# Merging the values and scores of the paired attention phase into one interruption of the feed-forward stream

## The chip, the cores and the metric

One core of one Trainium2 chip runs the whole program. The metric is the device time of one execution in microseconds (us). The median of three runs of the kernel before is 897.06 us (896.87 to 897.44). In the profiled execution TensorE had its full clock (2.4 GHz, granted clock 0.999).

## The reference

Banded attention over 8 batches, 8 heads, 576 positions and a head size of 64, followed by a two-layer feed-forward block with a leaky ReLU:

```python
scores = (1 / sqrt(64)) * q @ k.T          # [8, 8, 576, 576]
mask = (0 <= i - j) & (i - j < 64)         # each query sees itself and 63 keys before it
attn = softmax(where(mask, scores, -1e9))  # the sum has 1e-9 added
x = (attn @ v).transpose(0, 2, 1, 3).reshape(4608, 512)
h = x @ w_in                               # [4608, 2048]
out = maximum(0.01 * h, h) @ w_out         # [4608, 512]
```

All inputs and the output are float32.

## The kernel before, in words

**Units and pairs.** The 8 batches times 9 blocks of 64 queries are 72 units. A unit holds all 8 heads; it needs the 64 keys of its own block and the 64 before them. Two neighbouring units make a pair, numbered m = 0 to 35. Four pairs make one chunk of 512 rows of x, so there are nine chunks c = 0 to 8.

**The feed-forward stream.** For each chunk c and each of 16 tiles f of the hidden dimension, `mm1` (L532) computes h in 12 matmuls of 128x128 by 128x512: x and w_in are each split into a high and a low fp32r part, and three products are summed over four blocks of 128. It hands back three steps. `leak` (ScalarE, L544) writes the leaky ReLU g, `high` (ScalarE, L550) writes its high part gh, and `low` (VectorE, L554) writes gl = g - gh. `mm2` (L570) then adds gh and gl times w_out into four accumulator banks, 12 matmuls in four triples (gh, gh, gl). In the stream `mm2` of one step stands behind `mm1` of the next, so the three steps have the length of one `mm1` to finish. After f = 15 the four accumulators are evicted (L592) and stored.

**The paired phase.** Chunks 0 to 2 need pairs 0 to 11, which are done in earlier phases. From chunk 2 on a loop runs over n = 0 to 111, one (c, f) each. Pairs 12 to 35 are computed inside it, two pairs (m, m+1) in each eight steps, which I call a turn. TensorE leaves the stream twice per turn; I call each such interruption a visit:

- At the second step of a turn (at == 1): `scores_3` (L465) of both pairs. They are fp32 matmuls on 64x64 tiles of the array, two banks for each pair. `shield_3` (L470, VectorE) scales and masks them into e, `most_3` (L482, GpSimd) takes column maxima with partition_all_reduce, `exps_3` (L489) subtracts them (VectorE) and takes the exponential (ScalarE). The maximum of (m, 1) and that of (m+1, 0) are written to the two halves of `late_n`, the other two to a spare tile.
- At the third and fifth steps: exps of m+1, the sums by partition_all_reduce (L495, GpSimd; they too go to `late_n` and the spare tile), and `fold_3` (L499, VectorE), which makes reciprocals in `late_n`.
- At the sixth step (at == 5): `values_3` (L505) of both pairs, fp32 matmuls in 128x64 column tiles, one bank each ("s" for the even pair, "t" for the odd). `product_3` (L518) multiplies the bank by the reciprocals into `late_n` (VectorE) and copies the high part to x (ScalarE). `low_3` (L523, VectorE) writes the low part of x.

**Banks.** PSUM has eight banks: four accumulators o0 to o3, the two that `mm1` takes in turn ("o" and "h"), and "s" and "t". Before the change the scores of an even pair go to "s" and "t", those of an odd pair to "o" and "h".

**Order.** At the end a loop ties each instruction to the one written before it on the same engine ("issue order"). So every engine runs its instructions in the order of the program text; a wait at the head of an engine's queue holds all behind it. Tiles free their buffers by dependencies that the framework derives: a matmul that writes a bank waits until the last reader of its old content is done.

What stands in the loop at the visits of the kernel before:

```python
        if at == 5:
            for x in (m, m + 1):
                values_3(x)
                load_v(x + 2)
            product_3(m)
            fold_3(m + 1)
            low_3(m)
...
        if at == 1:
            for x in (m, m + 1):
                scores_3(x)
                load_q(x + 2)
```

Of the kernel before, what the change touches and what calls it, by code (L numbers as in the profile page):

```python
# [28 lines left out]
NU = B * NQB  # L29
# [5 lines left out]
PAIRED = 12  # L35
# [48 lines left out]
def flat(t):  # L84
    return t.rearrange("p a b -> p (a b)") if len(t.shape) == 3 else t
# [3 lines left out]
def band_attention_ffn(ctx: ExitStack, tc: tile.TileContext, qT, kB, vW, vL, w_in, w_out, eye_mask, out):  # L89
# [9 lines left out]
    def bank(tag, name):  # L99
        return ps_e.tile([P, 512], F32, tag=tag, name=name)  # L100


    of_h, of_a = cycle("oh"), cycle("st")
# [23 lines left out]
    def k_of(m):  # L127
        if m >= PAIRED:
            return (ks[0], later.get("k"), ks[1])[(m - PAIRED) % 3]
        return more[:, m] if m in (2, 3) else ks[m % 2]  # L130

    def v_of(m):
        if m >= PAIRED:
            return (vs[0], later.get("v"))[m % 2][:, :, : H * D]
        return vs[m % 2 if m < TURNED // 2 else 0][:, :, : H * (D + 1)]
# [8 lines left out]
    def load_k(m):  # L144
        if m < NU // 2:
            nc.sync.dma_start(k_of(m), kB[m])

    def load_v(m):
        if m < NU // 2:
            nc.sync.dma_start(v_of(m), vL[m - PAIRED] if m >= PAIRED else vW[m])  # L150
# [94 lines left out]
    def mask_of(u):  # L245

        kinds = [v % NQB == 0 for v in (u, u + 1)]
        if any(kinds):
            return away[:, 1:] if kinds[0] else away[:, :2]
        return away[:, :1]  # L250
# [204 lines left out]
    def open_room():  # L455

        e, n, v = (wk.tile([P, 512, 2], U32, tag="raw", bufs=3, name=f"late_{x}") for x in "env")
        e, n, v = (flat(x).bitcast(F32).rearrange("p (a b) -> p a b", a=2) for x in (e, n, v))
        k = flat(wk.tile([P, NP, 2, D], F32, tag="y", bufs=1, name="late_k").rearrange("p a b c -> p a (b c)"))
        later.update(e=e, n=n, v=v, k=k.rearrange("p (a b c) -> p a b c", a=UNITS, b=NP))  # L460

    def e_of(m):
        return (probs_of, later["e"])[m % 2]

    def scores_3(m):  # L465
        ps = [bank(t, f"s{m}_{j}") for j, t in enumerate((next(of_h), next(of_h)) if m % 2 else "st")]
        quarter_scores(m, ps, False)
        probs[m] = ps

    def shield_3(m):  # L470
        ps = probs.pop(m)
        a = mask_of(UNITS * m).bitcast(F32)
        n = a.shape[1]
        a = flat(a)[:, None, :].broadcast_to([P, H // n, n * QB])
        for j in range(2):
            e, s = (x.rearrange("a (b c) -> a b c", c=n * QB) for x in (e_of(m)[:, j], ps[j]))
            nc.vector.scalar_tensor_tensor(e, s, SCALE, a, ALU.mult, ALU.add)  # L477

    def spare(name):
        return wk.tile([P, 512], F32, tag="pT", bufs=1, name=name)  # L480

    def most_3(m):  # L482
        for j in range(2):
            b = 2 * (m % 2) + j
            mx = later["n"][:, b - 1] if b in (1, 2) else spare(f"mx{m}_{j}")
            nc.gpsimd.partition_all_reduce(mx, e_of(m)[:, j], P, ReduceOp.max)  # L486
            probs[m, j] = mx

    def exps_3(m):  # L489
        for j in range(2):  # L490
            e = e_of(m)[:, j]
            nc.vector.tensor_tensor(e, e, probs.pop((m, j)), ALU.subtract)  # L492
            nc.scalar.activation(e, e, AF.Exp)  # L493
# [5 lines left out]
    def fold_3(m):  # L499
        r, t = later["n"][:, m % 2], probs.pop((m, "sum"))  # L500
        nc.vector.tensor_scalar_add(r[64:], t[64:], 1e-9)
        nc.vector.tensor_scalar_add(r[:64], r[:64], 1e-9)
        nc.vector.reciprocal(r, r)  # L503

    def values_3(m):  # L505
        ps = bank("st"[m % 2], f"o{m}")
        for w in range(UNITS):
            v = v_heads(m, w)
            for p in range(NP):
                for j in range(2):  # L510
                    c = (2 * p + w) * QB
                    nc.tensor.matmul(  # L512
                        ps[64 * j : 64 * j + 64, c : c + QB], v[:, 2 * p + j], e_of(m)[:, j, c : c + QB],
                        start=True, stop=True,
                    )
        probs[m] = ps

    def product_3(m):  # L518
        r = later["n"][:, m % 2]
        nc.vector.tensor_tensor(r, probs.pop(m), r, ALU.mult)  # L520
        nc.scalar.copy(x_of(UNITS * m)[0], r.rearrange("a (b c) -> a b c", b=NP))

    def low_3(m):  # L523
        hi, lo = x_of(UNITS * m)
        t = later["n"][:, m % 2].rearrange("a (b c) -> a b c", b=NP)
        nc.vector.tensor_tensor(lo, t, hi.bitcast(F32), ALU.subtract)
# [5 lines left out]
    def mm1(c, f, part):  # L532

        xh, xl = xs[c]
        ps = bank(next(of_h) if c or f >= half else "h", f"h{c}_{f}_{part.start}")[:, part]
        wh, wl = wi[f]
        terms = [(a, b, k) for k in range(KT) for a, b in ((wh, xh), (wh, xl), (wl, xh))]
        for n, (a, b, k) in enumerate(terms):
            nc.tensor.matmul(ps, a[:, k, :], b[:, k, part], start=n == 0, stop=n == len(terms) - 1)  # L539
        t = []  # L540

        def leak():
            t.append(wk.tile([P, CH], F32, tag="g", bufs=1, name=f"g{c}_{f}_{part.start}")[:, part])
            nc.scalar.activation(t[0], ps, AF.Prelu, alpha=0.01)  # L544

        def high():
            g[c, f, part.start] = [
                wk.tile([P, CH], F32R, tag=n, name=f"{n}{c}_{f}_{part.start}") for n in ("gh", "gl")
            ]
            nc.scalar.copy(g[c, f, part.start][0][:, part], t[0])  # L550

        def low():
            hi, lo = (x[:, part] for x in g[c, f, part.start])
            nc.vector.tensor_tensor(lo, t[0], hi.bitcast(F32), ALU.subtract)  # L554

        return leak, high, low

    acc, sums, due = {}, {}, []
# [11 lines left out]
    def mm2(c, f, part):  # L570


        gh, gl = g.pop((c, f, part.start))
        wh, wl = wo[f]
        for i in range(part.start // P, part.stop // P):
            split = c == 1 or c == 0 and i < 2
            begin = f == 0 or split and f == half
            end = f == FT - 1 or split and f == half - 1
            if begin:
                pool, tag = (ps_o, f"o{i}")  # L580
                if c == 1 and f == 0 and i > 1:
                    pool, tag = ps_e, "st"[i - 2]
                acc[c, i] = pool.tile([P, DM], F32, tag=tag, name=f"acc{c}_{i}_{f}")
            ts = slice(i * P, (i + 1) * P)
            for n, (a, b) in enumerate(((gh, wh), (gh, wl), (gl, wh))):
                nc.tensor.matmul(  # L586
                    acc[c, i], a[:, ts], b, start=begin and n == 0, stop=end and n == 2
                )
            if end:
                due.append(partial(evict, c, i, f, split))  # L590
# [24 lines left out]
    def flush():  # L615
        while due:
            due.pop(0)()

    whole, first, second = slice(0, CH), slice(0, CH // 2), slice(CH // 2, CH)
# [40 lines left out]
    prev = jobs[-1]  # L660
    jobs = [(c, half + k, whole) for c in range(2) for k in range(half)]
    first_late = len(jobs) - UPC - 3
    for n, job in enumerate(jobs):
# [25 lines left out]
        prev = job  # L689

    open_room()
    load_k(PAIRED + 1)
    load_v(PAIRED + 1)
    steps = [(c, f) for c in range(2, NCHUNK) for f in range(FT)]
    for n, (c, f) in enumerate(steps):
        m = PAIRED + n // 8 * 2
        at = n % 8 if m < NU // 2 else None
        for step in mm1(c, f, whole):  # L700
            step()
        if at == 2:
            exps_3(m + 1)

            nc.vector.memset(later["n"][:1, 0, :1], 0.0)
            sums_3(m, 0)
            sums_3(m, 1)
            sums_3(m + 1, 0)
        if at == 4:
            fold_3(m)  # L710
            sums_3(m + 1, 1)
        if at == 5:
            for x in (m, m + 1):
                values_3(x)
                load_v(x + 2)
            product_3(m)
            fold_3(m + 1)
            low_3(m)
        if at == 6:
            product_3(m + 1)  # L720
            low_3(m + 1)
        if prev:
            mm2(*prev)
            flush()
        prev = (c, f, whole)
        if at == 1:
            for x in (m, m + 1):
                scores_3(x)
                load_q(x + 2)
            load_k(m + 2)  # L730
            load_k(m + 3)
            shield_3(m)
            shield_3(m + 1)
            most_3(m)
            exps_3(m)
            most_3(m + 1)
            mm2(*prev)
            flush()
            prev = None
# [61 lines left out]
```

## Time and profile before

| what | value |
|---|---|
| median of 3 runs | 897.06 us |
| profiled execution, its own time | 898.25 us |
| its span, first to last instruction | 896.5 us |
| TensorE matmuls busy | 887.8 us, 99% |
| VectorE busy | 498.6 us, 56% |
| ScalarE busy | 304.2 us, 34% |
| GpSimd busy | 315.1 us, 35% |
| DMA | 68.48 MB, mean 76 GB/s |

A row of the timeline gives the start, the duration, the engine, the line of the kernel, the operation, what it writes and reads, and how many equal neighbours were merged into the row. Times are us from the span's start. Matmuls overlap in the array: the start of one follows the start of the last by less than its duration, so distances are to be read from start to start. A bracket at the end tells how long the engine had been idle and what ended that.

### The profile page before, as it was taken

What the parts mean: (1) busy time and instruction counts of PE and PEld (TensorE: products, weight loads), DVE (VectorE), ACT (ScalarE), POOL (GpSimd) and SP (SyncE); (2) the same over time, 40 slices, a digit from 0 to 9 for tenths busy, and PEclk for the clock granted to TensorE, in tenths of its full rate; (3) what the DMA queues carried; (4) which work ended last, traced back from release to release, by engine and by line L of the source; (5) the groups of instructions that cost most, each with busy time, mean ns of one, the idle gap of its engine ahead of it and who ended that gap; (6) DMA issues with size and microseconds to landing.
All of it is one profiled execution on the core that took longest, in us unless ns stands there. A gap on an engine that the chain in (4) does not pass through costs nothing.

```text
span 896.5 us, 16193 instructions
## 1 busy us (share of the span) xinstructions
PE 887.8 (99%) x7018; PEld 730.0 (81%) x7018; DVE 498.6 (56%) x650; ACT 304.2 (34%) x517; POOL 315.1 (35%) x132
## 2 busy tenths in 40 slices
PE   8999999999999999999999999999999999999998
PEld 5887888888888888888888888888888888888886
DVE  7999774587473636455464737373636455461111
ACT  4666554232232333223322232223323322323222
POOL 5332000674351708071625335351708071620000
PEclk9999999999999999999999999999999999999999
DMA  9764633233311111012211121112101211001001
GB/s 317 216 211 120 222 89 123 72 101 128 116 48 36 59 50 59 35 48 71 72 48 48 48 95 48 48 49 89 53 4 59 81 48 48 2 1 48 0 1 48
DMA packets 30359, 68.48 MB, mean 76 GB/s; under 512 B 3024, under 2 KB 3152, under 8 KB 30288
## 3 DMA queue, kind: packets, MB, share of 16 engines
q1 hardware_dynamic: 25824, 51.75, 16.9%
q10 hardware_dynamic: 4464, 15.70, 5.9%
q8 instruction: 55, 0.90, 0.4%
q14 instruction: 16, 0.13, 0.0%
HBM read 56.43 MB, written 11.01 MB: 75 GB/s over the span
## 4 chain that ended last, share of the span: by engine, by line
PE 98%; issue 0%; POOL 0%; DMA 0%; ACT 0%; DVE 0%; ACTq 0%; DVEq 0%
PE acc L586 45%; PE h L539 44%; PE s L239 4%; PE o L512 3%; PE o L328 1%; DMA k<-kB 0%; PE s L273 0%; PE t L354 0%; PE o L424 0%; PE s L307 0%; POOL mx L293 0%; POOL room L293 0%; DVE s L603 0%; DVE e L283 0%; ACT e L314 0%
## 5 line engine op out<-in xcount | busy, mean ns | idle before, releaser
L539 PE MATMUL h<-x,wi 128*128 128x512 f32 (+1 forms) x1440 | 337.1, 384 | 0.5 <-ACT g L544 0.5
L539 PEld LDWEIGHTS h<-x,wi 128*128 128x128 f32 x1440 | 265.5, 188 | 54.5 <-ACT g L544 0.7
L586 PE MATMUL acc<-wo,gh 128*128 128x512 f32 x936 | 292.7, 394 | 0.5 <-DVE s L603 0.5
L554 DVE TENSOR_TENSOR gl<-g,gh 128x512 fp32r<-128x512 f32 (+1 forms) x147 | 107.5, 731 | 330.6 <-ACT gh L550 330.2
L586 PEld LDWEIGHTS acc<-wo,gh 128*128 128x128 f32 x936 | 172.8, 188 | 37.1 <-DVE s L603 0.7
L544 ACT ACTIVATE g<-h 128x512 f32<-128x512 f32 (+1 forms) x147 | 86.3, 587 | 328.8 <-PE h L539 325.2
L586 PE MATMUL acc<-wo,gl 128*128 128x512 f32 x468 | 182.5, 390 | 0.0
L486 POOL PARTITION_ALL_REDUCE mx<-e x12 | 21.4, 1782 | 307.0 <-DVE e L477 307.0
L586 PEld LDWEIGHTS acc<-wo,gl 128*128 128x128 f32 x468 | 87.8, 188 | 18.6
L550 ACT CAST gh<-g 128x512 fp32r<-128x512 f32 (+1 forms) x147 | 90.0, 612 | 10.6 <-PE acc L586 6.3
L503 DVE RECIPROCAL late_n<-late_n 128x512 f32<-128x512 f32 x24 | 80.5, 3352 | 0.8
L539 PE MATMUL h<-x,w 128*128 128x512 f32 x324 | 77.8, 389 | 0.0
L539 PEld LDWEIGHTS h<-x,w 128*128 128x128 f32 x324 | 60.8, 188 | 12.6
L586 PE MATMUL acc<-w,gh 128*128 128x512 f32 x216 | 66.7, 390 | 0.0
L497 POOL PARTITION_ALL_REDUCE late_n<-e x12 | 38.8, 3233 | 25.6 <-ACT late_e L493 25.6
L493 ACT ACTIVATE e<-e 128x512 f32<-128x512 f32 x24 | 15.2, 633 | 95.4 <-DVE e L492 95.4
L393 POOL PARTITION_ALL_REDUCE mx<-e x8 | 15.2, 1899 | 91.5 <-DVE e L385 88.2
L586 PEld LDWEIGHTS acc<-w,gh 128*128 128x128 f32 x216 | 40.5, 188 | 8.4
L586 PE MATMUL acc<-w,gl 128*128 128x512 f32 x108 | 42.0, 389 | 0.0
L293 POOL PARTITION_ALL_REDUCE mx<-e x13 | 25.7, 1978 | 45.1 <-ACT e L285 28.1
L497 POOL PARTITION_ALL_REDUCE n<-late_e x12 | 41.5, 3460 | 0.0
L497 POOL PARTITION_ALL_REDUCE late_n<-late_e x12 | 40.9, 3408 | 0.0
(99 smaller groups left out, 825.8 us busy)
## 6 DMA issues: line engine op xcount, KB each, us to landing
q<-qT SPq DMA_DIRECT2D x34, 256.0 KB, 3.5
raw<-w_out ACTq DMA_DIRECT2D x15, 512.0 KB, 3.6
out<-o SPq DMA_DIRECT2D x30, 256.0 KB, 2.1
raw<-w_in ACTq DMA_DIRECT2D x14, 512.0 KB, 3.7
k<-kB SPq DMA_DIRECT2D x25, 256.0 KB, 3.7
v<-vL SPq DMA_DIRECT2D x12, 512.0 KB, 3.8
late_v<-vL SPq DMA_DIRECT2D x12, 512.0 KB, 4.2
v<-vW SPq DMA_DIRECT2D x8, 520.0 KB, 5.3
```

Of the source, the lines that this page charges most:

```text
L239: nc.tensor.matmul(ps[j][t, c : c + QB], k[i][s, p], q[s, w, p], start=not begun and (not more or (w, p) == (0, 0)), stop=not begun and no ...
L293: nc.gpsimd.partition_all_reduce(mx, probs[b], P, ReduceOp.max)
L393: nc.gpsimd.partition_all_reduce(mx, probs_of[:, j], P, ReduceOp.max)
L486: nc.gpsimd.partition_all_reduce(mx, e_of(m)[:, j], P, ReduceOp.max)
L497: nc.gpsimd.partition_all_reduce(t, e_of(m)[:, j], P, ReduceOp.add)
L503: nc.vector.reciprocal(r, r)
L512: nc.tensor.matmul(ps[64 * j : 64 * j + 64, c : c + QB], v[:, 2 * p + j], e_of(m)[:, j, c : c + QB], start=True, stop=True,)
L539: nc.tensor.matmul(ps, a[:, k, :], b[:, k, part], start=n == 0, stop=n == len(terms) - 1)
L544: nc.scalar.activation(t[0], ps, AF.Prelu, alpha=0.01)
L550: nc.scalar.copy(g[c, f, part.start][0][:, part], t[0])
L554: nc.vector.tensor_tensor(lo, t[0], hi.bitcast(F32), ALU.subtract)
L586: nc.tensor.matmul(acc[c, i], a[:, ts], b, start=begin and n == 0, stop=end and n == 2)
```

## The change

One visit takes the values of two pairs and then the scores of the next two. The turns are shifted so that the visit stands two steps ahead of a multiple of eight (n = 14, 22, ..., 86). The first turn keeps its two visits (scores at n = 1, values at n = 5), n = 6 has scores alone, n = 94 values alone. The banks of the scores are exchanged: an even pair now takes "o" and "h", an odd pair "s" and "t", which the values of the visit have just filled. At f == 0 the call of `mm2` for the step before and two of its four evictions are written after the matmuls of `mm1` and ahead of its `leak`, `high` and `low`.

```diff
     def scores_3(m):
-        ps = [bank(t, f"s{m}_{j}") for j, t in enumerate((next(of_h), next(of_h)) if m % 2 else "st")]
+        ps = [bank(t, f"s{m}_{j}") for j, t in enumerate("st" if m % 2 else (next(of_h), next(of_h)))]
...
     for n, (c, f) in enumerate(steps):
-        m = PAIRED + n // 8 * 2
-        at = n % 8 if m < NU // 2 else None
-        for step in mm1(c, f, whole):
+        turn_of = (n + 2) // 8 if n > 5 else 0
+        m = PAIRED + 2 * turn_of
+        at = n - (8 * turn_of - 2 if turn_of else 1)
+        two = (m, m + 1) if m < NU // 2 else ()
+        mine = mm1(c, f, whole)
+        if f == 0:
+            mm2(*prev)
+            prev = None
+            for _ in range(2):
+                due.pop(0)()
+        for step in mine:
             step()
-        if at == 2:
+        flush()
+        if at == 1 and two:
             exps_3(m + 1)
...
-        if at == 4:
+        if at == 3 and two:
             fold_3(m)
             sums_3(m + 1, 1)
-        if at == 5:
-            for x in (m, m + 1):
+        if n == 5:
+            for x in two:
                 values_3(x)
                 load_v(x + 2)
             product_3(m)
             fold_3(m + 1)
             low_3(m)
-        if at == 6:
-            product_3(m + 1)
-            low_3(m + 1)
+        elif at == 5 and two:
+            fold_3(m + 1)
+        if n == 6:
+            product_3(m - 1)
+            low_3(m - 1)
         if prev:
             mm2(*prev)
             flush()
         prev = (c, f, whole)
-        if at == 1:
-            for x in (m, m + 1):
+        if at == 0 and m <= NU // 2:
+            done = (m - 2, m - 1) if turn_of > 1 else ()
+            for x in done:
+                values_3(x)
+                load_v(x + 2)
+            for x in two:
                 scores_3(x)
                 load_q(x + 2)
-            load_k(m + 2)
-            load_k(m + 3)
-            shield_3(m)
-            shield_3(m + 1)
-            most_3(m)
-            exps_3(m)
-            most_3(m + 1)
+            for x in two:
+                load_k(x + 2)
+            for x in done:
+                product_3(x)
+            for x in two:
+                shield_3(x)
+            for x in done:
+                low_3(x)
+            if two:
+                most_3(m)
+                exps_3(m)
+                most_3(m + 1)
             mm2(*prev)
             flush()
             prev = None
```

## Rows read from the trace of the kernel before

**Rows 1.** The page's chain that ended last, by engine.
```profile
PE 98%; issue 0%; POOL 0%; DMA 0%; ACT 0%; DVE 0%; ACTq 0%; DVEq 0%
```

**Rows 2.** Timeline of TensorE around a scores visit: start us, us, engine, line, operation.
```profile
429.27 0.39 PE L586 MATMUL acc<-wo,gl 128*128 128x512 f32 x1
429.59 0.27 PE L239 MATMUL s<-q,late_k 64*64 64x64 f32 x2
...
431.62 0.73 PE L586 MATMUL acc<-wo,gh 128*128 128x512 f32 x2
...
434.47 5.60 PE L539 MATMUL h<-x,wi 128*128 128x512 f32 x24
...
477.60 0.27 PE L239 MATMUL s<-q,k 64*64 64x64 f32 x2
```

**Rows 3.** Timeline of TensorE around the values visit of the same turn.
```profile
448.07 2.88 PE L539 MATMUL h<-x,wi 128*128 128x512 f32 x12
450.88 1.15 PE L512 MATMUL o<-e,v 128*64 128x64 f32 x32
451.87 1.10 PE L512 MATMUL o<-late_e,late_v 128*64 128x64 f32 x32
452.90 0.73 PE L586 MATMUL acc<-wo,gh 128*128 128x512 f32 x2
```

**Rows 4.** Timeline of TensorE in an earlier phase: values, then scores, of one pair.
```profile
171.14 1.15 PE L424 MATMUL o<-e,v 128*64 128x64 f32 x32
172.22 1.16 PE L239 MATMUL s<-q,k 64*64 64x64 f32 x64
173.31 0.74 PE L586 MATMUL acc<-w,gh 128*128 128x512 f32 x2
```

**Rows 5.** Timeline of VectorE behind the scores visit of rows 2.
```profile
430.80 1.29 DVE L477 SCALAR_TENSOR_TENSOR e<-s,away 128x512 f32<-128x512 f32 x2 [1.85 <-PE s L239]
432.01 1.28 DVE L477 SCALAR_TENSOR_TENSOR late_e<-s,away 128x512 f32<-128x512 f32 x2
433.48 1.53 DVE L492 TENSOR_TENSOR e<-e,mx 128x512 f32<-128x512 f32 x1 [0.19 <-POOL mx L486]
435.24 1.53 DVE L492 TENSOR_TENSOR e<-e,late_n 128x512 f32<-128x512 f32 x1 [0.23 <-POOL late_n L486]
438.74 0.69 DVE L554 TENSOR_TENSOR gl<-g,gh 128x512 fp32r<-128x512 f32 x1 [1.96 <-ACT gh L550]
```

**Rows 6.** Timeline of ScalarE behind the scores visit of rows 2.
```profile
436.81 0.63 ACT L493 ACTIVATE e<-e 128x512 f32<-128x512 f32 x1 [1.13 <-DVE e L492]
437.45 0.60 ACT L544 ACTIVATE g<-h 128x512 f32<-128x512 f32 x1
438.08 0.62 ACT L550 CAST gh<-g 128x512 fp32r<-128x512 f32 x1
```

**Rows 7.** Timeline of GpSimd behind the scores visit of rows 2.
```profile
431.66 1.78 POOL L486 PARTITION_ALL_REDUCE mx<-e  x1 [25.69 <-DVE e L477]
433.35 1.86 POOL L486 PARTITION_ALL_REDUCE late_n<-e  x1
```

**Rows 8.** Timeline of VectorE behind the values visit: product of one pair, low part of x.
```profile
454.74 0.68 DVE L520 TENSOR_TENSOR late_n<-o,late_n 128x512 f32<-128x512 f32 x1
...
462.13 0.69 DVE L526 TENSOR_TENSOR x<-late_n,x 128x512 fp32r<-128x512 f32 x1 [0.69 <-ACT x L521]
```

**Rows 9.** Timeline of GpSimd in the first phase: a maximum that starts beside VectorE.
```profile
49.86 2.15 POOL L293 PARTITION_ALL_REDUCE mx<-e  x1 [2.79 <-DVE sm L335]
```

**Rows 10.** Timeline of VectorE at the same moment.
```profile
49.68 0.68 DVE L194 SCALAR_TENSOR_TENSOR raw<-raw 128x512 uint32<-128x512 uint32 x1
```

**Rows 11.** Timeline of ScalarE: the exponential that the values of rows 4 wait for.
```profile
170.28 0.63 ACT L399 ACTIVATE e<-e 128x512 f32<-128x512 f32 x1 [3.16 <-DVE e L398]
```

**Rows 12.** Timeline of ScalarE at a chunk's end: third and fourth eviction.
```profile
329.42 1.25 ACT L612 COPY o<-acc 128x512 f32<-128x512 f32 x2 [1.69 <-DMA out<-o]
```

**Rows 13.** DMA issues by kind, count, KB each, us to landing: the slowest load of this phase.
```profile
late_v<-vL SPq DMA_DIRECT2D x12, 512.0 KB, 4.2
```

## The prediction

> **What bounds the kernel now.** The first view is the chain of waits that ended last: 98% of it is TensorE [rows 1]. So the time is the length of TensorE's instruction stream, and anything else counts only where it makes TensorE wait. The second view is TensorE's timeline over one turn, read from start to start. Behind the scores visit, 24 matmuls take 5.60 us with 0.39 us for the last one alone, so a matmul of the stream follows the one before by (5.60 - 0.39) / 23 = 0.2267 us [rows 2]. A step has 24 of them, 5.44 us, and eight steps 43.52 us. From one scores visit to the next the trace has 477.60 - 429.59 = 48.01 us [rows 2]. The two visits of a turn thus cost 4.49 us, and if both can be accounted for by themselves, nothing else stalls TensorE in a turn. The third view is the timelines of the other three engines behind the scores visit [rows 5 to 7], for what a moved visit will meet.
>
> **What one visit costs.** Scores: from the last matmul of the stream (429.27) to the next one (431.62) are 2.35 us. Less the 0.227 us of an ordinary step from one to the next, that is 2.12. The first `mm2` behind it runs from 431.62 to 434.47, 2.85 instead of 2.72, so 0.13 more [rows 2]: 2.25 in all. Values: the last matmul of `mm1` starts at 448.07 + 2.88 - 0.39 = 450.56, the next of the stream at 452.90: 2.34 - 0.23 + 0.13 = 2.24 [rows 3]. Together 4.49, which is what the period left over. So the turn has no hidden stall that the change could remove.
>
> **The merged visit.** The early phase has values followed directly by scores, for one pair: 32 value matmuls take 171.14 to 172.22, 1.08 us, where 32 followed by more values take 451.87 - 450.88 = 0.99. The change of tile shape inside a visit so costs 0.09 us. The 64 score matmuls up to the next matmul of the stream take 1.09 us [rows 3, 4]; the other 64 of a visit of two pairs take 431.62 - 429.59 - 1.09 = 0.94 [rows 2]. The merged visit: 0.32 from the last matmul of the stream to the first value (450.88 - 450.56), 0.99 and 1.08 for the values, 0.94 and 1.09 for the scores, less 0.23, plus 0.13: 4.32 us. Against 4.49 a merger saves 0.17 to 0.18 us, I take 0.175.
>
> The loop before makes 24 visits. The new one makes 14: n = 1, 5 and 6, ten merged ones at n = 14 to 86, and n = 94. Ten mergers give 10 x 0.175 = **1.75 us**. The bounds: no gain if the inner change of shape cost as much as leaving and entering the stream, and 10 x 0.26 = 2.6 us if it cost nothing.
>
> **What the merged visit meets.** I set t = 0 at its first value matmul and let every engine run in the order of the text. Take n = 14, with values of pairs 14 and 15 and scores of 16 and 17.
>
> *TensorE.* Values 14 from 0, values 15 from 0.99, scores 16 from 2.07, scores 17 from 3.01, the stream again at 4.10. Then `mm2`(14) to 6.95, `mm1`(15) to 9.67, `mm1`(16) to 12.39. There `mm2`(15) starts, and its third matmul, the first that needs gl, is due 0.45 later at 12.84.
>
> *The exchanged banks.* Scores 17 write "s" and "t", so they wait for both products. The values of a pair take 1.15 and 1.10 us [rows 3], a product 0.68 [rows 8]. From the start of 64 scores to VectorE's reading them are 430.80 - 429.59 = 1.21 us [rows 2, 5], which is 0.05 behind the last one's end. Product 14 so ends near 1.9, product 15 near 0.99 + 1.10 + 0.05 + 0.68 = 2.82. From ScalarE's end to a waiting matmul are 171.14 - 170.91 = 0.23 us [rows 4, 11]; with that "t" is usable at 3.05 against 3.01. I take 0.02 per visit, 0.2 us in all. The bounds are 0, where the weight load is not held up, and 0.3 per visit, where product 15 starts a third of a microsecond late.
>
> *VectorE.* Four shields follow, the first pair 3.28 to 4.57, the second 4.49 to 5.77 (1.29 and 1.28 for two [rows 5]). Before the change the subtractions came next. Now the two `low_3` do, 0.69 each [rows 8]: 5.70 to 6.39 and 6.31 to 7.00.
>
> *GpSimd.* Maximum (16, 0) starts 0.21 behind its shield (430.80 + 0.65 to 431.66) [rows 5, 7], here 4.14, and ends at 5.92. Maximum (16, 1) writes the half of `late_n` that `low_3`(14) reads, so it waits for that: 6.39 + 0.21 = 6.60. Before the change it followed its predecessor without a gap, 433.35, which is 1.73 behind the visit's end [rows 2, 7]; now it is 2.50 behind. It also starts while `low_3`(15) has 0.40 to run. Another such start, with 0.50 left of a VectorE instruction of two SBUF inputs, took 2.15 instead of 1.78 [rows 7, 9, 10]. I read this as a delay of what is left less 0.13, here 0.27: the maximum ends at 6.60 + 1.78 + 0.27 = 8.65.
>
> *The chain to gl.* Subtraction (16, 1) runs beside the next maximum and takes 1.53, as both do in [rows 5]: 8.69 to 10.22. Its exponential ends at 10.89 (0.63 [rows 6]). `leak`(15) is behind it on ScalarE. Its matmuls end near 9.85, so before this there was nothing to wait for; now it runs 10.90 to 11.50, `high` to 12.15, `low` 12.19 to 12.88 (0.60, 0.62, 0.69 [rows 5, 6]). With 0.23 to the matmul [rows 4, 11] it is 13.11, and a little more for the wider weight load, against 12.84. TensorE waits **0.3 us** in each merged visit, 3.0 us in all. Before the change the same chain was 0.77 earlier against the visit's end, and `leak` started within a tenth of when h was done. The bounds: nothing, if the maximum runs as if alone (gl then at 12.6), and 0.9 per visit if `low_3` itself is held up beside a maximum as the subtractions are (1.53 - 0.69 = 0.84 [rows 5, 8]).
>
> **The other edits**, each with its cover:
>
> - At f == 0 the matmuls of `mm1` are still written before those of `mm2`, since the call of `mm1` issues them. TensorE's order at a chunk's boundary is unchanged. Two evictions now come ahead of `leak`(16) on ScalarE. They take 0.62 each [rows 12] and wait for the first two accumulators. By the clock above `leak` starts near 15.9 instead of 12.6, and gl(16) is ready near 17.8; `mm2`(16) is due at 18.1. The third eviction still waits for a store (1.69 [rows 12]); it is ahead of `leak`(17), whose gl has till 23. Cost 0; were the cover gone, some tenths of a microsecond at six boundaries.
> - `fold_3` of the even pair now has no values visit behind it to hide gl of the next step. The sums start 0.8 us later than before, because the memset ahead of them follows the subtractions. By the same clock gl(18) is ready near 28.1 and due at 29.5. Cost 0, at most 0.5 per turn.
> - x of pairs 14 and 15 is complete at 7.0, and `mm1`(16) starts at 9.67. Cost 0.
> - The loads of v now start beside those of q and k on SP's queue, ahead of the chunk's stores. The slowest lands in 4.2 us [rows 13], the next visit is 43 us away. Cost 0.
> - n = 6 has scores alone, five steps after n = 1 and one after the values at n = 5; product 13 is done some 0.5 us after the scores begin, before the bank "t" is reached. Cost 0 to 0.3 once.
>
> **Sum.** 898.25 - 1.75 + 0.2 + 3.0 = 899.7 us for an execution like the profiled one. The median of the runs is 1.19 below the profiled execution, so I forecast 898.5 us, 0.16% above before. A measurement of this kernel can tell about 0.2% from no change, 1.8 us.
>
> **Rivals.**
>
> - *No wait.* Maximum (16, 1) is not held up by `low_3`(15); gl is ready near 12.6, within the cover. Only the mergers are left: 897.06 - 1.75 = 895.3, up to 896.5 with remnants. For it: the margin is a few hundredths. Against it: the stretched maximum in [rows 9].
> - *The shared reads hold VectorE longer (the slower side).* `low_3`(14) comes up at 5.70, while maximum (16, 0) runs to 5.92. If it must wait for the end, 5.92, it ends 0.22 later, and so does the whole chain to gl: 0.52 in each visit, 10 x 0.52 - 1.75 + 0.2 = +3.7, 900.7 us; with the full 0.84 on it, 1.14 per visit and 906.9. It decides from the point where gl is more than 0.18 late per visit. Against it: the subtraction that started at 433.48 ended at 435.01, while the maximum that began at 433.35 ended at 435.21 [rows 5, 7], so VectorE had its data before the end. The Trainium skill (SBUF — State Buffer, Who interferes with whom) says that a VectorE instruction with two SBUF inputs and a GpSimd instruction that reads SBUF exclude each other, whoever is first, for the whole instruction. By that rule the wait to 5.92 is what happens; the rows just named agree with an exclusion but not with one that lasts the whole instruction.
> - *The banks.* Product 15 is late for scores 17 by 0.3: 10 x 0.3 beside the forecast's other terms, 901.3 us. Against it: VectorE is idle when the visit begins.
> - *The mergers bring more.* With the inner change of shape free and no wait, 897.06 - 2.6 = 894.5.
> - *It does not do what it says*: the visits could be counted otherwise. The indices give 14, so I set this aside.
>
> **Chances.** The forecast's mechanism with a wait of 0.1 to 0.45 per visit (896.6 to 900.2): 0.43. No wait: 0.27. Shared reads: 0.20. Banks: 0.05. More: 0.05. Faster by over 0.2% means under 895.3: the last one and a third of "no wait", 0.15. Slower means over 898.9: shared reads, banks and the upper third of the forecast, 0.40. Within: 0.45. The range of 8 in 10 reaches from 895.1, which holds nearly all of "no wait", to 902.5, which holds the smaller of the shared-read cases; the forecast alone has 896.6 to 900.2.
>
> **What would show it.** The merged visit from the last matmul of the stream ahead to the first behind should be 4.42 us, and 1.08 or so from the second values to the scores. Maximum (m, 1) should start right behind `low_3` of the even done pair and take about 2.05. `leak` of the step behind the visit should start about 0.8 to 1.0 late behind an exponential, and a gap of about 0.3 us should stand between the second and the third matmul of the second `mm2` behind each merged visit. The forecast is wrong if that gap is absent or near a microsecond, if a gap stands between the two scores, or if one appears at f == 0.

## The result and the profile after

The changed kernel takes 899.9 us (median of 6 runs, 898.95 to 900.6) against 897.5 (896.87 to 897.65): ratio 1.0028, interval 1.0018 to 1.0038. It is slower by 2.4 us, in the range that was forecast and on its side. The reason is for the most part another one, so the agreement is luck.

The profiled execution took 900.34 us, its span is 898.5. The page's chain by engine, to set beside [rows 1]:

```profile
PE 97%; DVE 2%; issue 1%; DMA 0%; ACT 0%; ACTq 0%; DVEq 0%
```

TensorE still sets the time. VectorE's 2% lie in the first 50 us, ahead of the loop. "issue" is time in which the engine waits for nothing that the profile shows; over the whole span it is 0.6% of the chain after and 0.5% before, but between 240 and 800 us it is 0.5% after and nothing before. First a merged visit as it was meant. The timeline of TensorE at n = 22 (to set beside [rows 2 and 3]; start us, us, engine, line, operation):

```profile
361.82 0.39 PE L586 MATMUL acc<-wo,gl 128*128 128x512 f32 x1
362.14 1.15 PE L512 MATMUL o<-e,v 128*64 128x64 f32 x32
363.12 1.10 PE L512 MATMUL o<-late_e,late_v 128*64 128x64 f32 x32
364.16 1.21 PE L239 MATMUL s<-q,k 64*64 64x64 f32 x66
...
366.18 0.50 PE L586 MATMUL acc<-wo,gh 128*128 128x512 f32 x1
```

From 361.82 to 366.18 are 4.36 us; 4.42 were forecast, and 1.03 to 1.04 us instead of 1.08 from the second values to the scores. Five of the ten merged visits have this length. The other five look like n = 54:

```profile
555.42 1.10 PE L512 MATMUL o<-late_e,late_v 128*64 128x64 f32 x32
...
556.92 1.62 PE L239 MATMUL s<-q,k 64*64 64x64 f32 x97
559.44 0.27 PE L239 MATMUL s<-q,k 64*64 64x64 f32 x1 [0.90 <-issue]
559.63 0.74 PE L586 MATMUL acc<-wo,gh 128*128 128x512 f32 x2
```

Just before the last matmul of the scores TensorE stops for 1.12 us from start to start, in the midst of equal matmuls on equal tiles, and the profile shows nothing that releases it. The granted clock was 1.00 from 554 to 560 us, so the clock is not the reason. The five such visits take 5.52, 4.79, 5.46, 4.99 and 4.69 us, 3.65 more than five of 4.36. The two visits ahead of them (n = 38 and 46) have the same kind of wait in the first `mm2` behind, 0.34 and 0.43 us. Together 4.4 us. The waits of TensorE between 300 and 800 us, after and then before (us in total, times, longest; PE is a matmul, PEld a weight load; the rows that name `o` stand at the begin of each values visit in both):

```profile
PEld o L512 <- issue: 3.9, 11, 0.4
PEld s L239 <- issue: 2.9, 5, 1.0
...
PE s L239 <- issue: 2.0, 3, 0.9
...
PEld acc L586 <- issue: 1.0, 2, 0.6
PEld acc L586 <- DVE gl L554: 0.6, 3, 0.2
PE acc L586 <- issue: 0.4, 2, 0.3
```

```profile
PEld o L512 <- issue: 3.9, 11, 0.4
PEld s L239 <- issue: 3.5, 10, 0.4
```

Before, a wait for "issue" in this stretch is never longer than 0.4 us and stands only where the tile shape changes. After, it reaches 1.0, and the wait for gl that was to cost 3 us stands there three times only.

**Where these waits lie.** Count all matmuls and weight loads of TensorE in order of their start, from 0. The seven waits come at numbers 8081, 8847, 9611, 10375, 11139, 11905 and 12669 of the trace after. The steps are 764 or 766, which is 3 x 256 less 2 or 4. The page has 55 packets of one instruction queue for TensorE's 2 x 7018 instructions, 255 for each packet:

```profile
PE 888.6 (99%) x7018; PEld 732.2 (81%) x7018; DVE 500.0 (56%) x650; ACT 303.0 (34%) x517; POOL 318.4 (35%) x132
...
q8 instruction: 55, 0.90, 0.4%
```

0.90 MB in 55 packets are 16 KB each, 64 bytes for an instruction. So TensorE's program comes in blocks of 256 instructions, and each of the waits stands where one block ends and the next begins. Two things in the trace bear this out. Take the first instruction held up at each wait (in four of the seven it is the weight load just ahead of the matmul counted here), and count the 75 semaphore and drain instructions of TensorE's queue too: then the steps from wait to wait are exactly 768, three blocks. And in each case a 16 KB packet of that queue began 2.3 to 2.9 us before the wait ended. The 256 instructions ahead of a wait began 2.4 to 3.15 us before it ended (the start of instruction number 8081 - 256, and so on). In the stream 256 instructions last 128 x 0.227 = 29 us; in the scores they last 2.0 us. A turn has 768 counted instructions, three blocks. The few that are not counted move the border by 2 or 4 per turn, from behind the visit into its end: hence nothing in the first three merged visits, a wait behind the next two, and one inside the last five. The Trainium skill (Runtime: NRT & Kernel Launch, Instruction fetch mechanics) says that an engine's instructions come in blocks of 16 KiB, 256 instructions, fetched while the block before runs, and that the cost of a border is mostly hidden. The size agrees with the 16 KB here; "hidden" does not hold for a visit of 384 instructions in 4 us.

**The chain to gl**, as the prediction set it up, at n = 22. VectorE (to set beside [rows 5 and 8]), GpSimd [rows 7], ScalarE [rows 6]:

```profile
363.37 0.69 DVE L520 TENSOR_TENSOR late_n<-o,late_n 128x512 f32<-128x512 f32 x1 [1.86 <-PE o L512]
364.27 0.69 DVE L520 TENSOR_TENSOR late_n<-o,late_n 128x512 f32<-128x512 f32 x1 [0.21 <-PE o L512]
365.37 1.29 DVE L477 SCALAR_TENSOR_TENSOR e<-s,away 128x512 f32<-128x512 f32 x2 [0.40 <-PE s L239]
...
367.77 1.28 DVE L526 TENSOR_TENSOR x<-late_n,x 128x512 fp32r<-128x512 f32 x2
...
370.73 1.53 DVE L492 TENSOR_TENSOR e<-e,late_n 128x512 f32<-128x512 f32 x1 [0.23 <-POOL late_n L486]
374.17 0.69 DVE L554 TENSOR_TENSOR gl<-g,gh 128x512 fp32r<-128x512 f32 x1 [1.90 <-ACT gh L550]
```

```profile
366.23 1.78 POOL L486 PARTITION_ALL_REDUCE mx<-e  x1 [24.82 <-DVE e L477]
368.55 2.15 POOL L486 PARTITION_ALL_REDUCE late_n<-e  x1 [0.54 <-DVE x L526]
```

```profile
372.36 0.63 ACT L493 ACTIVATE e<-e 128x512 f32<-128x512 f32 x1 [1.14 <-DVE e L492]
372.90 0.58 ACT L544 ACTIVATE g<-h 128x512 f32<-128x512 f32 x1
373.51 0.62 ACT L550 CAST gh<-g 128x512 fp32r<-128x512 f32 x1
```

With t = 0 at 362.14 each step comes where it was put or up to 0.2 us earlier: the second maximum waits for `low_3`, starts at 6.41 (forecast 6.60), is stretched to 2.15 (2.05), gl ends at 12.72 (12.88). But TensorE loses only 0.06 to 0.07 us by it, seen where the third matmul of `mm2` is followed at 0.30 instead of 0.23:

```profile
327.06 0.46 PE L586 MATMUL acc<-w,gl 128*128 128x512 f32 x1
327.35 0.62 PE L586 MATMUL acc<-w,gh 128*128 128x512 f32 x2
```

### The profile page after: what moved, and what is told of

The parts are those of the page before. It is cut to its first block, busy times and chain, and to the rows that moved or that the text cites. A ratio compares the mean times of both kernels' runs of the same rounds, so it can differ in the third digit from the quotient of the medians.

```text
span 898.5 us, 16209 instructions
## 1 busy us (share of the span) xinstructions
PE 888.6 (99%) x7018; PEld 732.2 (81%) x7018; DVE 500.0 (56%) x650; ACT 303.0 (34%) x517; POOL 318.4 (35%) x132
## 4 chain that ended last, share of the span: by engine, by line
PE 97%; DVE 2%; issue 1%; DMA 0%; ACT 0%; ACTq 0%; DVEq 0%
PE acc L586 44%; PE h L539 44%; PE s L239 4%; PE o L512 3%; PE o L328 1%; DMA k<-kB 0%; PE o L424 0%; PE t L354 0%; DVE raw L190 0%; PE s L273 0%; DVE w L207 0%; DVE raw L194 0%; DVE raw L202 0%; DVE e L283 0%; DVE wo L214 0%
## 5 line engine op out<-in xcount | busy, mean ns | idle before, releaser
L554 DVE TENSOR_TENSOR gl<-g,gh 128x512 fp32r<-128x512 f32 (+1 forms) x147 | 105.0, 714 | 329.6 <-ACT gh L550 329.2
```

## The experiments

Theory A: the loss is TensorE's instruction blocks, used up before the next is there. Theory B: it is gl, as forecast. Theory C: a bank or a load. Each median stands beside 897.4 to 897.6 for the kernel before on the same chip.

**e1: the blocks shifted.** 198 more instructions at the start, where TensorE waits for its first load (`Y` in the order calls `pad`; each of its small matmuls is two matmuls and two weight loads in the trace):

```diff
-q0 X6 S0 ...
+q0 X1 Y52 S0 ...
...
+    def pad(n):
+        ps = [bank(t, f"pad{j}") for j, t in enumerate("ho")]
+        w = flat(wi[half + 4][0]).bitcast(F32)
+        for a in range(n):
+            i, j = a // 2 % 2, a % 2
+            s, t = slice(64 * j, 64 * j + 64), slice(64 * i, 64 * i + 64)
+            nc.tensor.matmul(ps[j][t, :QB], w[s, :QB], w[s, :QB], start=True, stop=True)
```

> The changed kernel with 198 more TensorE instructions (52 small matmuls of 64x64, for five of the six idle matmuls) before the first scores, where TensorE waits for its first load. They shift every later visit against the blocks of 256 instructions in which the trace shows TensorE's instructions being fetched. Theory A (in seven of the merged visits TensorE has used up a block before the next is there): the block's border moves to where only one falls into a visit, the gaps of 0.3 to 1.1 us at the end of the scores and in the matmuls behind go, about 4.5 us; some 895.3 us, 0.25% below before. Theory B (gl is late behind a merged visit, 0.3 us each, as forecast): nothing moves, 899.9. Theory C (the waits are for a bank or for a load of q, k or v): nothing moves either.

896.94 us, ratio 0.9996 (0.9988 to 1.0005). All ten merged visits take 4.36 us. TensorE's waits between 300 and 800 us:

```profile
PEld o L512 <- issue: 3.9, 11, 0.4
...
PEld acc L586 <- DVE gl L554: 2.1, 10, 0.2
```

The waits for "issue" are gone but for those that were there before, and now gl is waited for in all ten. Ahead of the loop nothing but 198 instructions was added, and the loads and banks of the visits are as they were, so theory C does not give this; theory A does. No packet of instructions began in a visit now: each began 4.1 us or more behind the first value matmul, against 1.8 to 2.3 us for the seven waits. The run also shows that B exists and is small. The median is 1.6 us above the expected 895.3, by B and by what e8 shows.

**e2: the kernel before with its blocks shifted.** `X6` becomes `X3 Y32`, 122 instructions.

> The kernel before with 122 more TensorE instructions at the same place. The border of a block, which falls into the middle of each scores visit, should come to its first instructions, and the next border 256 instructions and 2.0 us behind, at its end. Theory A: blocks took 2.4 to 3.2 us from border to first use, so each of the 12 scores visits waits 0.4 to 1.1 us: 902 to 910 us, although nothing is merged. Theories B and C: 897.5, as before.

897.95 us, ratio 1.0008 (0.9999 to 1.0016), no wait in any visit. The expectation missed: a scores visit of 256 instructions alone did not use up its block at this place. The trace has a packet that began 0.4 to 3.1 us ahead of each visit's first matmul and the next one not before 2.7 us after it. Read by theory A, the fetch that has to be done when the visit ends, 2.0 us on, was under way before the visit began and had at least 2.4 us. That fits A but does not test it as was meant, and only this place was tried.

**e3: the loads moved off the visit.** `True` sends a load from ScalarE's queue.

```diff
             for x in done:
                 values_3(x)
-                load_v(x + 2)
             for x in two:
                 scores_3(x)
-                load_q(x + 2)
-            for x in two:
-                load_k(x + 2)
...
+        if at == 2 and m <= NU // 2:
+            for x in done:
+                load_v(x + 2, True)
...
```

> The changed kernel with the loads of v, q and k of a merged visit issued two steps later from ScalarE's queue, so that they do not run beside the visit. If the 2.4 to 3.2 us from a block's border to its first use are long because the loads take the DMA engines, they fall to about 2.1 and most of the 4.5 us of gaps goes: 895.5 to 897. If a fetch takes that long by itself, 899 to 900.5, with gaps of the same size.

899.49 us, ratio 1.0029 (1.0017 to 1.0041). The five visits lose 2.8 us instead of 3.65, and from 256 instructions ahead to the end of a wait are 2.4 to 2.9 us, 2.6 in the mean against 2.8. So most of the time is there without the loads. Whether they lengthen it is not shown: the means differ by less than the waits do among themselves. ScalarE's queue now issues the loads ahead of `leak` (one wait of 3.4 us before it), and TensorE's waits for gl are 1.0 us in all instead of 0.6. The median does not differ from the changed kernel's 899.9 clear of its scatter.

**e4: a smaller shift.** `X6` becomes `X4 Y20`, 76 instructions.

> The changed kernel with 76 more TensorE instructions at the start (20 small matmuls for two idle ones). The two borders in a merged visit move 76 instructions towards its begin, where the slower value matmuls are: the 256 instructions between them then take 2.6 to 2.9 us instead of 2.1 to 2.4. Theory A: gaps of 0 to 0.5 us remain in the ten visits, in the middle of the second pair's scores: 896 to 898.5 us. Theories B and C: 899.9.

899.5 us, ratio 1.0022 (1.0013 to 1.0032). The waits moved forward in the visit as theory A has it: counted with the semaphores and drains, the five large ones leave the same remainder by 256 as the seven of the changed kernel, 193, though 76 instructions more stand ahead. They came in the first merged visits too, here n = 14, ahead of the last 30 matmuls of the scores:

```profile
317.92 0.32 PE L239 MATMUL s<-q,k 64*64 64x64 f32 x4
318.50 0.69 PE L239 MATMUL s<-q,k 64*64 64x64 f32 x30 [0.25 <-issue]
```

Their size was underrated: 0.14 to 0.86 us in six of the ten visits, none in four. The 256 instructions ahead of them took 2.6 to 3.4 us here, up to the end of the wait. How long a fetch takes differs from one to the next; its parts stand in the last section.

**e5: one `low_3` ahead of the shields**, on top of e1.

```diff
+            for x in done[:1]:
+                low_3(x)
             for x in two:
                 shield_3(x)
-            for x in done:
+            for x in done[1:]:
                 low_3(x)
```

> The shifted kernel of e1 with the first of the two low_3 written ahead of the shields instead of behind them, so that the maximum that writes over its late_n half need not wait for it. e1 shows a gap of 0.06 to 0.075 us at the first gl of the second mm2 behind each of the ten merged visits, and matmuls some hundredths late behind it. If gl is what they wait for, the chain of maximum, subtraction, exponential, leak is some 0.4 us earlier and the gaps go: 0.7 us below e1, 896.2. If the gaps have another cause, no change: 896.9.

896.06 us, ratio 0.9984 (0.9975 to 0.9992): the first whose interval lies wholly below the kernel before. VectorE and then GpSimd at n = 22 (values start at 362.71):

```profile
365.44 0.68 DVE L526 TENSOR_TENSOR x<-late_n,x 128x512 fp32r<-128x512 f32 x1
366.04 1.28 DVE L477 SCALAR_TENSOR_TENSOR e<-s,away 128x512 f32<-128x512 f32 x2
```

```profile
366.90 1.78 POOL L486 PARTITION_ALL_REDUCE mx<-e  x1 [25.33 <-DVE e L477]
368.58 2.18 POOL L486 PARTITION_ALL_REDUCE late_n<-e  x1
```

The second maximum follows the first without a gap, and the rows of gl are gone from TensorE's waits. From one merged visit to the next are 47.81 us, against 47.90 in e1 and 48.01 before: gl cost 0.09 us per turn, and a merger with neither wait brings 0.20.

**e6: the edit at f == 0 undone**, on top of e1 (the block `if f == 0` and the `flush()` behind the steps taken out).

> The shifted kernel of e1 with the edit at f == 0 undone (mm2 of the step before and all four evictions behind leak, high and low, as in the kernel before). The prediction held this edit to cost nothing; a rival is that two evictions ahead of leak cost some tenths of a microsecond at each of seven chunk borders. Expected with the former 896.9 as in e1, with the latter 895 to 896. The waits that TensorE's queue carries may be other ones, so the border of a block may drift differently.

896.79 us, ratio 0.9995 (0.9986 to 1.0004); the turn stays at 47.90. The edit costs nothing that this can measure.

**e7: the banks not exchanged**, on top of e1 (the line of `scores_3` as before).

> The shifted kernel of e1 with the banks of the scores as before (even pair s and t, odd pair o and h). The even pair's scores stand right behind the values and then wait for the second product. By the prediction's clock that is ready at 2.82 and 0.1 to 0.2 on the way, against a start at 2.07: 0.8 to 0.9 us in each of ten visits, 905 to 906 us, and the exchange of banks is what keeps the product off the path. If TensorE runs on for lack of a real conflict, 896.9.

905.75 us, ratio 1.0093 (1.008 to 1.0107). The merged visit takes 5.22 us, 0.86 more. TensorE, then VectorE at the sixth of them; the second product ends at 561.63:

```profile
561.68 0.27 PE L239 MATMUL s<-q,late_k 64*64 64x64 f32 x1 [0.54 <-DVE late_n L520]
```

```profile
560.94 0.69 DVE L520 TENSOR_TENSOR late_n<-o,late_n 128x512 f32<-128x512 f32 x1 [0.22 <-PE o L512]
```

With the banks exchanged the second pair's scores follow the first's after 0.98 us, as in a visit that waits for nothing: the exchange hides the product wholly.

**e8: control**, the kernel before with e1's addition.

> Control: the kernel before with the 198 added instructions of e1. If the addition itself costs or brings nothing, 897.4 as before; then the 0.5 us that e1 is below before comes from the merged visits. If it changes the early phase by some tenths, this shows how much.

898.15 us, ratio 1.0008 (1.0 to 1.0017). By the medians the addition costs 0.7 us. Its matmuls run past the time at which the first scores could have started (4.62 before):

```profile
2.29 3.05 PE L644 MATMUL pad<-wi 64*64 64x64 f32 x104
5.12 1.81 PE L239 MATMUL s<-q,k 64*64 64x64 f32 x64
```

Whether that is all of the 0.7 is not shown: in e5's trace, for one, TensorE also stops for 1.0 us at 10.42 for "issue", amid scores of the first phase. So e1 is to be held against 898.15: 1.2 us below, and e5 2.1 us below. Ten turns shorter by 0.11 and 0.20 us make 1.1 and 2.0. The traces agree without the start: from the first paired scores to the end are 658.93 us before and in e8, 657.87 in e1, 656.90 in e5.

**e9: e5 with a shorter addition** (`X1 Y40`, 150 instructions).

> As e5, with 150 instead of 198 added instructions (40 small matmuls), so that the addition ends before the first load is there: in the traces of e1, e5 and e8 it ran until 5.1 us, against 4.62 where the first scores start without it. The border then lies 214 to 242 instructions into a merged visit; the block before it has at least 3.8 us. Theory A: no gaps in the visits, the turn at 47.81 us as in e5, and 0.3 to 0.5 us less at the start: 895.5 to 895.8. If the place needs more distance than that, some gaps come back and it is above 896.1.

895.95 us, ratio 0.9982 (0.9973 to 0.9991). The merged visits are all 4.36 us, and the start is free:

```profile
2.29 2.41 PE L644 MATMUL pad<-wi 64*64 64x64 f32 x80
4.48 1.25 PE L239 MATMUL s<-q,k 64*64 64x64 f32 x64
```

It brought a tenth of a microsecond more, not the 0.3 to 0.5 expected, so the late start of the first scores is a small part of what the addition cost. Why the rest is there is open. This is the best version of the study: 1.6 us below the kernel before and 4.0 below the changed one.

## Why the prediction came out, step by step

The time lay in the range, but by luck: two errors of the sum went against each other. It had -1.75 for the mergers and +3.2 for waits of gl and of the banks. The profile has this instead:

- **The mergers.** Forecast 0.175 us each. With all waits removed (e5) a turn is 0.20 shorter, 2.0 in all. The step was right; the inner change of shape was a little dearer in the row of one pair, 1.08, than in a visit of two, 1.03.
- **The banks.** Forecast 0.02 per visit; nothing is seen, and without the exchange it is 0.86 (forecast 0.8 to 0.9 for e7). Right.
- **The chain to gl.** The mechanism is right in every link, and the stretched maximum came as [rows 9] had it. The size was wrong: 0.09 per turn (e1 less e5) instead of 0.30. gl came 0.16 us earlier than by the prediction's clock, and from its end to the weight load that takes it were 0.05 us and to the matmul 0.09, where the prediction had put 0.23. In the changed kernel itself it is worth less still, three times 0.06 to 0.07, because the other visits were late anyway.
- **The covers** of the edit at f == 0 (e6), of `fold_3`, of x and of the banks held; no wait stands there.
- **The step that failed** is the first of the prediction's clock, TensorE's: "Values 14 from 0, ..., the stream again at 4.10". It took for granted that TensorE always has its next instructions. Before the change no visit had more than 256 in a row; the merged one has 384, and in seven of ten the next block was not there: 4.4 us, a term that the sum did not have and no rival named. The forecast put the loss down to a wait for gl; it was the supply of instructions, shown by e1 (waits gone when the blocks' place was moved), e4 (waits moved with it) and the packets that began 2.3 to 2.9 us before each wait ended.
- A slip without effect: (5.60 - 0.39) / 23 is 0.2265, not 0.2267; a step stays 5.44 us.

Added up from the first paired scores visit to the end, the trace after is 2.9 us longer than before: -2.1 for ten mergers without waits, +4.4 for the blocks, +0.2 for gl, and 0.3 to 0.4 in matmuls some hundredths late behind the visits. The early phase, which the change leaves alone, happened to be 0.8 us shorter in this execution, which makes the 2.0 between the spans.

Of the rival that VectorE is held by GpSimd's maximum for all its length: the `low_3` at 367.77 came beside the maximum that began at 366.23 and both together took 1.28 us, as if alone. By the row of GpSimd they overlapped for 0.24 us; the wait to the maximum's end that this rival had at this place did not come.

## What to carry to other kernels

Count instructions, not only microseconds, where many small matmuls are put in a row: 64x64 tiles use up 256 instructions in 2 us, and the next block was there only after 2.4 to 3.4 in the waits seen here. A wait for "issue" amid equal matmuls, at distances that are multiples of 256 instructions, tells of it, and some added instructions in an idle place ahead move it. And a forecast that hits the time has not thereby found the cause: it was found only by looking at where the gaps lie.

## What the runs showed of the hardware that was not expected

- The kernel's time depends on where its instructions fall in blocks of 256: 198 small matmul instructions in an idle stretch at the start took 3 us off the changed kernel (899.9 to 896.94).
- From the first of 256 instructions to the use of the next block were 2.4 to 3.4 us in the 19 waits measured (after, e3, e4). The traces split this in three: up to 0.8 us until the packet began, 0.9 to 1.4 us for the packet itself, and 1.25 to 1.55 us from its end to the end of the wait. So the last part hardly varies, and the first two make the difference. What sets them is open.
- Single runs scattered more with waits of this kind: 898.95 to 900.6 for the changed kernel, 895.79 to 896.14 for e9.
